# k's maximum over the partitions by TensorE transposes in the first three batches of an attention and feed-forward kernel

## The chip, the cores and the metric

The kernel runs on one core of a Trainium2 chip. The metric is device time in microseconds (us) of one execution. Engines carry the profile's names: PE is TensorE, DVE VectorE, ACT ScalarE, POOL GpSimd, SP SyncE (here the queue that issues every DMA). Each works through its own instructions in their order and waits on semaphores for the others.

## The reference

Linear attention, then a feed-forward block with softplus. q's softmax runs along each head's 64 columns, k's along the 576 rows of the sequence, and it is k's maximum over those rows that this case is about. The random inputs are scaled before use, q by 22.844, k, v and w_in by 8.

```python
batch, n_heads, seq, head_dim = (8, 8, 576, 64)
k_s = k - np.max(k, axis=2, keepdims=True)
k_s = np.exp(k_s)
k_s = k_s / (np.sum(k_s, axis=2, keepdims=True) + 1e-09)
kv = np.einsum('bhsd,bhse->bhde', k_s, v)
...
h = x @ w_in                     # x [4608, 512], w_in [512, 2048]
g = np.maximum(h, 0.0) + np.log1p(np.exp(-np.abs(h)))
return (g @ w_out).astype(np.float32)
```

## The kernel before

The 4608 tokens are cut into 12 tiles of 384, d_ff into 16 chunks of 128. One (tile, chunk) pair is a **slot**, and the 192 slots set the order of everything. In a slot TensorE makes `up` (x times a chunk of w_in, into PSUM tile `ph`), then `down` of two slots before (g times a chunk of w_out, into `po`), then what `later` has put aside: products of k and v and of x. ScalarE and VectorE make the softplus between (L405 to L411). Tile 0 takes the weights as float32; the other tiles take weights and x in two float32r parts (`hi` and `lo`), three products each.

The weights come as 32 loads of 512 KB of float64 bits and are made float32 on the chip, two chunks per slot of tile 0: GpSimd scales them (`scale_w`, L161), ScalarE takes the top bits (L166), VectorE the sign (L170) and the join (L177). From slot 6 on ScalarE (L190) and GpSimd (L191) also split two chunks per slot, into the place of chunks that tile 0 has used.

A `kv_unit` makes one head pair of one batch: `top` takes the maximum of k over the chunks (VectorE, tile `mx`) and then over the 128 partitions, the same result in every partition (GpSimd's `partition_all_reduce`, tile `mb`); `shift` subtracts it, on GpSimd for two head pairs of the first batch and for all units that tiles 1 and 2 plan, on VectorE else; `product` takes the exponential and multiplies by v and a column of ones; `scale` and `split` divide. x of a tile is `flip` (a 32x32 block transpose of q), `product` and `split`.

Before the first slot these steps stand in an order written out by hand (the string of names such as `u00` for step 0 of head pair 0, `q1`, `x00`, `w3`). In the slots a `Plan` places them: each step has a cost by engine, each unit a first slot (`KV_AT`) and a number of slots to wait after the step before, and the least room per slot that lets all fit is taken. Units of batch 1 are made in the slots of tile 0, two of batch 2 in tile 1. `kv_prefetch` loads the next head pair into one of two buffers once the products of an earlier one are done. All DMAs stand in SP's queue in program order; the load of tile 1's q (`q`) stands ahead of the weights from the fourth chunk on (`w3` and later), and waits until tile 0's q has been used.

Of the kernel before, what the change touches and what calls it, by code (L numbers as in the profile page):

```python
# [6 lines left out]

# [9 lines left out]
P = 128  # L17
B, H, S, D = 8, 8, 576, 64
DM, DF = 512, 2048
NT = B * S  # L20
HP = H // 2          # head pairs: one pair fills the 128 partitions
NJ = DF // P
NCH = S // P         # whole chunks of the sequence, plus one of half the rows
# [3 lines left out]
W_SCALE = 2.0**8     # what the weights on chip are scaled by  # L27
SPARE = 2            # see the weights

# Tiles of tokens of the feed-forward part, in blocks of 128. The first takes the weights as float32,  # L30
# while they are still being converted; the others take them, and all else, in two parts for float32r.
SUBS = [3] * 12
# From which slot (see slots()) the weights are split, and how many chunks of them in a slot.
SPLIT_FROM, SPLITS = 6, 2
# The slot from which the second tile's attention part is made.
ATT_FROM = 3
# When a tile comes to the products of k and v that it makes for the next, by their number.
KV_AT = {0: (), 1: (4,), 2: (2, 8), 3: (1, 5, 9), 4: (0, 2, 4, 6)}
# [10 lines left out]
def segments(t):  # L49
    """(batch, first column, last column) of the tokens of tile t."""  # L50
    out, a = [], START[t]
    while a < START[t + 1]:
        b = a // S
        e = min((b + 1) * S, START[t + 1])
        out.append((b, a - START[t], e - START[t]))
        a = e
    return out


def slots():  # L60
    """The order in which (tile, chunk of d_ff) go through the tensor engine."""
    return [(t, j) for t in range(NTILE) for j in range(NJ)]


class Plan:
    """Gives the steps of the work beside the feed-forward products their slots."""
# [6 lines left out]
    def place(self, unit, first, last, room):  # L73
        """Puts the steps of a unit, (slots to wait after the step before, cost by engine, function), where
        there is room for them, and returns their slots, or None."""
# [15 lines left out]
    def place_all(self, attempt):  # L91
        """attempt(plan, room) with the least room that does."""
# [11 lines left out]
def tile_attn_ffn(  # L104
    ctx: ExitStack,
    tc: tile.TileContext,
    q: bass.AP,       # [128, HP * NT]  tile after tile, in blocks of 32 x 32, see kernel()
    kv: bass.AP,      # [B, HP, 128, NCH, 2, 2 * D]  k and v of each head side by side
    kv_tail: bass.AP, # [B, HP, 64, 2, 2 * D]
    w_in: bass.AP,    # [NJ, 128, DM]  float64 as its 64 bits  # L110
    w_out: bass.AP,   # [NJ, 128, DM]  likewise
    out: bass.AP,     # [NT, DM]
# [20 lines left out]
    zero = const.tile([P, 1], F32, name="zero")  # L133
    ln1 = const.tile([P, 1], F32, name="ln1")

    # ---------------------------------------------------------------- weights
    # The weights of a chunk come as float64, and become float32 where they are. The first tile is made
    # from these. Then their two parts for float32r take the place of the chunk SPARE before.
# [12 lines left out]
    # A float64 has its sign, 11 bits of exponent and 20 of the fraction in the high word. Read as a  # L151
    # float32, scaled by 2^-111 and shifted left by 3, that word is the float32 of W_SCALE times the
    # value's magnitude without the fraction's last 3 bits, which are the top of the low word.
# [4 lines left out]
    def scale_w(i):  # L158
        """The high words, read as float32, by 2^-111."""
        _, high = words(i, F32)  # L160
        nc.gpsimd.tensor_scalar(out=high, in0=high, scalar1=2.0**-60, scalar2=2.0**-51, op0=ALU.mult, op1=ALU.mult)  # L161

    def top_w(i):
        """The low words' top 3 bits: the whole part of a 32nd of the top byte, to which the conversion rounds."""
        low, _ = words(i, U32)
        nc.scalar.activation(low, octets(i)[:, :, 3], AF.Copy, scale=1.0 / 32, bias=-15.5 / 32)  # L166

    def sign_w(i):
        """The sign, from the high words' top byte to that of the low words."""
# [4 lines left out]
    def join_w(i):  # L174
        """The float64 weights times W_SCALE, cut to float32, in the place of their low words."""
# [5 lines left out]
    def whole(i):  # L181
        """The weights of a chunk as float32, among the words that they came in."""
        return words(i, F32)[0]

    def split_w(i):
        """The two parts for float32r."""
# [7 lines left out]
    # ------------------------------------------------- k softmax and its product with v  # L194
    waiting = None  # where products that need not come at once are put
# [7 lines left out]
    KVW = 2 * D + 1  # a head's columns of k, its columns of v, a column of ones  # L203

    def kv_load(b, h, pool=kp, tag="kvt", shape=(P, NCH + 1, 2, KVW)):
# [3 lines left out]
        # Rows that the last chunk does not have: no maximum, weight 0.  # L209
# [9 lines left out]
    def kv_unit(b, h, ps, engine=nc.vector, after=None):  # L219
        """exp(k - max)' [v, 1] for one head pair, divided by its last column, as kv_hi and kv_lo."""  # L220
        t = loaded.pop((b, h))
        kt, vt = t[:, :, :, 0:D], t[:, :, :, D:KVW]
        ps = ps[:, 0:D + 1]
        state = {}

        def top():
            mx = sm.tile([P, 2, D], F32, name="mx")
            nc.vector.tensor_reduce(out=mx, in_=kt.rearrange("p c z d -> p z d c"), op=ALU.max, axis=AX.X)  # L228
            mb = sm.tile([P, 2, D], F32, name="mb")
# [5 lines left out]

        def shift():
            engine.tensor_tensor(
# [38 lines left out]
        return [top, shift, product, scale, split]  # L276

    def split_kv(h):
        """The two parts of a head pair's product in the first batch, which the first tile takes whole."""
# [3 lines left out]
    # ------------------------------------------------------------- q softmax, x  # L283
# [8 lines left out]
    def swapped(m):  # L292
        """The same columns of the other 32 partitions of the head."""
# [6 lines left out]
    def q_unit(t):  # L300
        """Softmax of q of tile t, two head pairs at a time."""
# [35 lines left out]
    def x_unit(t, h, ps, tiles=None):  # L337
        """x of a head pair, columns on the partitions and scaled by 1 / W_SCALE, in two parts but for tile 0."""
# [44 lines left out]
    # ------------------------------------------------------------ feed-forward  # L383
# [15 lines left out]
    def softplus(ph, t):  # L399
        """max(h, 0) + log1p(u), u = exp(-|h|); log1p(u) = ln(w) + (u - (w - 1)) with w = 1 + u."""  # L400
# [44 lines left out]
    def finish(t, m):  # L445
        """Writes out 128 tokens, after tile 0 by way of the places of the last weights that came."""
# [12 lines left out]
    # ---------------------------------------------------------------- schedule  # L459
# [12 lines left out]
    with tc.manual_schedule():  # L472
        # Before the first products much of what they need is free for their inputs to be made.
# [5 lines left out]
        for i in range(3):  # L479
            load_w(i)  # L480
        nc.vector.memset(zero, 0.0)
        # What the table gives for ln(1), so that log1p is exact where 1 + u rounds to 1.
# [6 lines left out]
        def place(h, at):  # L489
            """PSUM for a unit, in one of two banks."""  # L490
            return (more if h % 2 else att)[:, at:512]

        # Its parts step by step, in the order that lets every engine work: u for k and v, q, x and k
        # (split_kv) with their head pair and step, s and the like for the weights with their chunk.
# [16 lines left out]
        for name in (  # L511
# [152 lines left out]
```

## Time and profile before

| what | value |
|---|---|
| median of 3 runs | 1007.84 us (1007.72 to 1008.45) |
| profiled execution, its span | 1005.5 us |
| busy in the span | PE 90%, DVE 74%, ACT 61%, POOL 14% |
| first feed-forward product | 51.67 us |
| first product of tile 1 | 201.73 us |
| GpSimd's reductions | 32, from 7.28 us to 831.9 us |

The profile shows one execution. Its span runs from the first to the last recorded instruction; the time of a run lies a little above it. A bracket behind a row tells how long the engine had been idle and what ended that; "issue" means that the profile shows nothing it waited for. The page cuts the span into 40 slices of 25.1 us, the digit being the busy share in tenths: the first eight differ from all that follow.

```profile
PE   0297553889899999999999999999999999999998
DVE  7195566868678888788689788687888887676554
POOL 1322347434100000001000000001000000000000
PEclk9998875998999999999999999999999999999999
```

### The profile page before, as it was taken

Reading aid. Unit: us, or ns where it says so; the run is one execution under the profiler, and the core shown is the slowest. Engines: PE = TensorE matmul, PEld = TensorE weight load, DVE = VectorE, ACT = ScalarE, POOL = GpSimd, SP = SyncE. Lnnn points to the kernel's source line nnn. Section 1 sums busy time; section 2 is a strip of 40 time slices with the busy share of each in tenths; the row PEclk is TensorE's granted clock in tenths of the full one; section 3 lists DMA queues with packets and bytes.
Section 4 is the critical chain, followed back from the end, with each engine's and each line's share of the span. In section 5 each row is a group of like instructions: output and inputs, shape, how many; then the busy total and the mean of one; then the engine's idle time right before and its main releaser. Section 6 shows DMA issues by size and latency. Waiting matters only on the chain.

```text
span 1005.5 us, 13226 instructions
## 1 busy us (share of the span) xinstructions
PE 901.8 (90%) x4748; PEld 768.1 (76%) x4748; DVE 746.1 (74%) x1369; ACT 616.1 (61%) x1262; POOL 138.1 (14%) x205
## 2 busy tenths in 40 slices
PE   0297553889899999999999999999999999999998
PEld 0143222468798988989989888988988989999997
DVE  7195566868678888788689788687888887676554
ACT  2263334557566666676676676676667666666654
POOL 1322347434100000001000000001000000000000
PEclk9998875998999999999999999999999999999999
DMA  8273330100011101100110110110102001000000
GB/s 235 73 314 108 107 107 24 32 32 25 24 64 48 55 33 48 56 32 24 55 56 24 56 55 24 57 55 24 63 25 79 32 25 32 33 1 1 31 1 32
DMA packets 49473, 55.37 MB, mean 55 GB/s; under 512 B 2304, under 2 KB 39168, under 8 KB 49408
## 3 DMA queue, kind: packets, MB, share of 16 engines
q1 hardware_dynamic: 49408, 54.54, 16.6%
q8 instruction: 37, 0.61, 0.2%
q14 instruction: 28, 0.23, 0.1%
HBM read 45.09 MB, written 9.44 MB: 54 GB/s over the span
## 4 chain that ended last, share of the span: by engine, by line
PE 77%; issue 7%; DVE 6%; POOL 4%; DMA 3%; ACT 1%; SPq 0%; POOLq 0%; DVEq 0%
PE ph L394 12%; PE ph L396 12%; PE ph L395 12%; PE po L440 12%; PE po L441 12%; PE po L439 12%; DMA w<-in_w_in 3%; POOL w L191 2%; DVE w L177 1%; POOL w L161 1%; DVE w L170 1%; PE po L248 1%; PE po L435 1%; PE att L248 1%; DMA qt<-in_q 1%
## 5 line engine op out<-in xcount | busy, mean ns | idle before, releaser
L439 PE MATMUL po<-w,g_hi 128*128 128x512 f32 x528 | 206.5, 391 | 5.3 <-ACT g_hi L419 5.2
L394 PE MATMUL ph<-x_hi,w 128*128 128x384 f32 x616 | 210.4, 342 | 0.0
L441 PE MATMUL po<-w,g_lo 128*128 128x512 f32 x528 | 209.8, 397 | 0.0
L440 PE MATMUL po<-w,g_hi 128*128 128x512 f32 x528 | 209.3, 396 | 0.0
L396 PE MATMUL ph<-x_lo,w 128*128 128x384 f32 x616 | 208.0, 338 | 0.0
L395 PE MATMUL ph<-x_hi,w 128*128 128x384 f32 x616 | 207.2, 336 | 0.0
L409 DVE SCALAR_TENSOR_TENSOR w<-w,u 128x384 f32<-128x384 f32 x192 | 112.3, 585 | 126.7 <-ACT w L407 124.7
L419 ACT CAST g_hi<-l 128x384 fp32r<-128x384 f32 x176 | 90.5, 514 | 170.9 <-DVE l L411 170.6
L405 ACT ACTIVATE u<-ph 128x384 f32<-128x384 f32 x192 | 94.3, 491 | 60.7 <-PE ph L396 28.8
L410 DVE SCALAR_TENSOR_TENSOR u<-ph,w 128x384 f32<-128x384 f32 x192 | 107.1, 558 | 21.3 <-ACT q_hi L355 0.5
L394 PEld LDWEIGHTS ph<-x_hi,w 128*128 128x128 f32 x616 | 116.1, 188 | 5.7 <-issue 0.3
L395 PEld LDWEIGHTS ph<-x_hi,w 128*128 128x128 f32 x616 | 116.1, 189 | 4.4 <-issue 0.3
L439 PEld LDWEIGHTS po<-w,g_hi 128*128 128x128 f32 x528 | 99.7, 189 | 21.8 <-ACT g_hi L419 6.0
L441 PEld LDWEIGHTS po<-w,g_lo 128*128 128x128 f32 x528 | 99.4, 188 | 21.8 <-DVE g_lo L420 0.5
L396 PEld LDWEIGHTS ph<-x_lo,w 128*128 128x128 f32 x616 | 116.0, 188 | 0.0
L411 DVE SCALAR_TENSOR_TENSOR l<-l,ln,u 128x384 f32<-128x384 f32 x176 | 110.1, 625 | 6.3
L420 DVE TENSOR_TENSOR g_lo<-l,g_hi 128x384 fp32r<-128x384 f32 x176 | 97.6, 555 | 22.8 <-ACT g_hi L419 20.7
L440 PEld LDWEIGHTS po<-w,g_hi 128*128 128x128 f32 x528 | 99.6, 189 | 16.8
L406 ACT ACTIVATE u<-u 128x384 f32<-128x384 f32 x192 | 100.9, 526 | 6.1
L407 ACT ACTIVATE w<-u 128x384 f32<-128x384 f32 x192 | 100.8, 525 | 6.1
L230 POOL PARTITION_ALL_REDUCE mb<-mx x32 | 32.1, 1003 | 418.5 <-DVE mx L228 348.3
L408 ACT ACTIVATE l<-u 128x384 f32<-128x384 f32 x176 | 89.3, 508 | 0.0
(111 smaller groups left out, 1085.8 us busy)
## 6 DMA issues: line engine op xcount, KB each, us to landing
kvt<-in_kv SPq DMA_DIRECT2D x30, 512.0 KB, 4.3
qt<-in_q SPq DMA_DIRECT2D x12, 768.0 KB, 4.2
out<-w SPq DMA_DIRECT2D x33, 256.0 KB, 2.2
w<-in_w_in SPq DMA_DIRECT2D x16, 512.0 KB, 8.1
w<-in_w_out SPq DMA_DIRECT2D x16, 512.0 KB, 7.9
kvt<-in_kv_tail SPq DMA_DIRECT2D x30, 64.0 KB, 3.9
out<-x_lo SPq DMA_DIRECT2D x3, 256.0 KB, 3.2
x_hi<-in_kv SPq DMA_DIRECT2D x1, 512.0 KB, 8.5
```

The lines of the kernel that those rows point to most:

```text
L394: nc.tensor.matmul(ph, lhsT=w_hi, rhs=x_hi[:, h], start=h == 0, stop=False)
L395: nc.tensor.matmul(ph, lhsT=w_lo, rhs=x_hi[:, h], start=False, stop=False)
L396: nc.tensor.matmul(ph, lhsT=w_hi, rhs=x_lo[:, h], start=False, stop=h == HP - 1)
L406: nc.scalar.activation(u, u, AF.Exp, scale=-1.0)
L407: nc.scalar.activation(w, u, AF.Copy, bias=1.0)
L409: nc.vector.scalar_tensor_tensor(out=w, in0=w, scalar=1.0, in1=u, op0=ALU.subtract, op1=ALU.subtract)
L410: nc.vector.scalar_tensor_tensor(out=u, in0=ph, scalar=0.0, in1=w, op0=ALU.max, op1=ALU.subtract)
L411: nc.vector.scalar_tensor_tensor(out=l, in0=l, scalar=ln1, in1=u, op0=ALU.subtract, op1=ALU.add)
L420: nc.vector.tensor_tensor(out=g_lo, in0=l, in1=g_hi.bitcast(F32), op=ALU.subtract)
L439: nc.tensor.matmul(po, lhsT=g_hi[:, ms], rhs=w_hi, start=j == 0, stop=False)
L440: nc.tensor.matmul(po, lhsT=g_hi[:, ms], rhs=w_lo, start=False, stop=False)
L441: nc.tensor.matmul(po, lhsT=g_lo[:, ms], rhs=w_hi, start=False, stop=j == NJ - 1)
```

## The change

For batches 0 to 2 (`b <= ON_PE`) the maximum over the partitions is no longer taken on GpSimd. TensorE transposes `mx` into PSUM with an identity matrix, so that partitions become columns; VectorE takes the maximum of each row (`m1`, one column); TensorE transposes `m1`, read 128 times over, which puts all maxima into every partition. `shift` reads them from PSUM where VectorE does it; for GpSimd, ScalarE copies them into SBUF first. The middle piece is a new step, `across`, so the numbers of the later steps go up by one; for batches from 3 on it does nothing. The identity is made once on GpSimd. The order ahead of the first slot is written anew, and four units of a tile now begin at slots 0, 1, 4 and 5 instead of 0, 2, 4 and 6. Comments are also gone, which moves line numbers.

```diff
-KV_AT = {0: (), 1: (4,), 2: (2, 8), 3: (1, 5, 9), 4: (0, 2, 4, 6)}
+ON_PE = 2
+KV_AT = {0: (), 1: (4,), 2: (2, 8), 3: (1, 5, 9), 4: (0, 1, 4, 5)}
...
+    ident = const.tile([P, P], F32, name="ident")
...
-        ps = ps[:, 0:D + 1]
+        wide, ps = ps[:, 0:P], ps[:, 0:D + 1]
...
             nc.vector.tensor_reduce(out=mx, in_=kt.rearrange("p c z d -> p z d c"), op=ALU.max, axis=AX.X)
+            if b <= ON_PE:
+                later(lambda: nc.tensor.transpose(wide, mx.rearrange("p z d -> p (z d)"), ident))
+                return
             mb = sm.tile([P, 2, D], F32, name="mb")
             nc.gpsimd.partition_all_reduce(
...
+        def across():
+            if b > ON_PE:
+                return
+            m1 = sm.tile([P, 1], F32, name="m1")
+            nc.vector.tensor_reduce(out=m1, in_=wide, op=ALU.max, axis=AX.X)
+            later(lambda: nc.tensor.transpose(wide, m1.broadcast_to([P, P]), ident))
+
         def shift():
+            if b <= ON_PE:
+                mb = wide.rearrange("p (z d) -> p z d", z=2)
+                if engine is nc.gpsimd:
+                    mb = sm.tile([P, 2, D], F32, name="mb")
+                    nc.scalar.copy(mb.rearrange("p z d -> p (z d)"), wide)
+                state["mb"] = mb
...
-        return [top, shift, product, scale, split]
+        return [top, across, shift, product, scale, split]
...
+        make_identity(nc, ident)
...
-            "u00 u01 u10 q1 q0 u11 u12 q2 u20 q3 u21 q4 u30 u02 u13 q6 m2 q5 u03 t0 t2 q7 q9 u22 m1 u14 "
-            "q8 x00 x10 u31 x11 u32 u04 x30 x20 kv m0 s0 u33 x01 t1 s2 u23 u34 u24 x12 x31 kv s1 q w3 w4 "
-            "w5 w6 w7 j1 k0 k3 j0 j2 x02 m3 x32 x21 t3 t4 x22 k1 k2 m4"
+            "u00 u10 u01 u11 u20 u02 u21 u12 u30 u31 q0 q1 u22 u32 u03 u13 q2 m0 q3 m1 u04 u14 q4 u05 u15 "
+            "t0 q5 m2 t1 q6 u23 u33 q7 q9 q8 x00 u24 u34 x01 x10 x11 u25 u35 t2 x20 x30 kv s0 x21 x31 kv "
+            "j0 x02 x12 s1 q w3 w4 w5 w6 w7 j1 x22 x32 k0 k1 s2 m3 k2 k3 j2 t3 t4 m4"
...
                 costs = [
-                    (0, dict(dve=0.8, pool=1.3)), (1, dict(dve=0.75)), (1, dict(act=0.75)), (1, dict(dve=0.2)),
-                    (1, dict(dve=0.4, act=0.4)),
+                    (0, dict(dve=0.8, pool=1.3)), (1 if b <= ON_PE else 0, dict(dve=0.2 if b <= ON_PE else 0)),
+                    (1, dict(dve=0.75)), (1, dict(act=0.75)), (1, dict(dve=0.2)),
+                    (0 if b <= ON_PE else 1, dict(dve=0.4, act=0.4)),
                 ]
```

What the order of instructions becomes is shown at three places, before and then now. First GpSimd ahead of the first slot; `ISA mb<-mx` is the reduction, a bare `ISA` a change of configuration, `mb` and `mx` as above, `w_136` to `w_141` the first weights.

```order
L230 ISA
L230 ISA mb<-mx 128x128 x3
L237 ISA
L237 TENSOR_TENSOR x_hi<-x_hi,mb 128x10x64
L230 ISA
L230 ISA mb<-mx 128x128
L161 ISA
L161 TENSOR_SCALAR w_140<-w_140 128x512
L330 TENSOR_TENSOR qt<-qt,s 128x768
L161 TENSOR_SCALAR w_138<-w_138 128x512
L237 TENSOR_TENSOR x_lo<-x_lo,mb 128x10x64
```

```order
masks.py:197 MEMSET ident 128x128
masks.py:199 ISA
masks.py:199 AFFINE_SELECT ident<-ident 128x128
L258 TENSOR_TENSOR x_hi<-x_hi,mb 128x10x64
L258 TENSOR_TENSOR x_lo<-x_lo,mb 128x10x64
L165 TENSOR_SCALAR w_137<-w_137 128x512
L165 TENSOR_SCALAR w_139<-w_139 128x512
L165 TENSOR_SCALAR w_141<-w_141 128x512
L351 TENSOR_TENSOR qt<-qt,s 128x768
```

Four bare ISA rows have become one, ahead of the identity, and the subtractions, scalings and the multiply follow each other.

Second, VectorE at the same place (`m` and `m_171` are different tiles: the maxima of q, and the new column).

```order
L228 TENSOR_REDUCE mx<-kvt 128x128
L237 TENSOR_TENSOR kvt<-kvt,mb 128x10x64
L228 TENSOR_REDUCE mx<-kvt 128x128
L311 TENSOR_REDUCE m<-qt 128x24 x2
L237 TENSOR_TENSOR kvt<-kvt,mb 128x10x64
L297 COPY other<-m 32x48 x4
L314 TENSOR_TENSOR m<-m,other 128x48
L228 TENSOR_REDUCE mx<-x_hi 128x128
L317 TENSOR_TENSOR qt<-qt,m 128x768 x2
L228 TENSOR_REDUCE mx<-x_lo 128x128
```

```order
L232 TENSOR_REDUCE mx<-kvt 128x128 x2
L248 TENSOR_REDUCE m_171<-po_159 128x1
L248 TENSOR_REDUCE m_174<-po_160 128x1
L232 TENSOR_REDUCE mx<-x_hi 128x128
L258 TENSOR_TENSOR kvt<-kvt,po_159 128x10x64
L248 TENSOR_REDUCE m_181<-po_161 128x1
L258 TENSOR_TENSOR kvt<-kvt,po_160 128x10x64
L232 TENSOR_REDUCE mx<-x_lo 128x128
L248 TENSOR_REDUCE m_188<-po_162 128x1
L332 TENSOR_REDUCE m<-qt 128x24 x2
```

All four head pairs' maxima now stand ahead of the work on q.

Third, TensorE in tile 0, where batch 1 is made (`ph` is `up`, `po_415` and `po_432` and on `down`; `att` and `po_332` or `po_349` are the two banks of the units).

```order
L389 MATMUL ph<-x_hi,w_311 128x384 x4
L435 MATMUL po_415<-w_309,g_hi 128x512
L435 MATMUL po_416<-w_309,g_hi 128x512
L435 MATMUL po_417<-w_309,g_hi 128x512
L389 MATMUL ph<-x_hi,w_336 128x384 x4
L435 MATMUL po_415<-w_334,g_hi 128x512
L435 MATMUL po_416<-w_334,g_hi 128x512
L435 MATMUL po_417<-w_334,g_hi 128x512
L248 MATMUL att<-kvt 64x65 x10
```

```order
L234 MATMUL att<-ident,mx 128x128
L410 MATMUL ph<-x_hi,w_330 128x384 x4
L456 MATMUL po_432<-w_328,g_hi 128x512
L456 MATMUL po_433<-w_328,g_hi 128x512
L456 MATMUL po_434<-w_328,g_hi 128x512
L249 MATMUL att<-ident,m_483 128x128
L234 MATMUL po_349<-ident,mx 128x128
L410 MATMUL ph<-x_hi,w_353 128x384 x4
```

At the end of slots 3 to 5 TensorE's queue now has transposes, each behind a `mx` or `m1` of VectorE; the first head pair's products come at the end of slot 6, where they came at the end of slot 5.

More of the change, by code (lines that the diff above doesn't have):

```diff
@@ L6 @@
 from concourse._compat import with_exitstack
+from concourse.masks import make_identity
 F32 = mybir.dt.float32
```

## The prediction

> **What bounds the kernel now.** I read the profiled execution by stages first: up to the first feed-forward product, tile 0, and the rest.
>
> ```profile
> core 0: us, PE busy (x) PEld busy (x) DVE busy (x) ACT busy (x) POOL busy (x), PEclk, DMA share, GB/s
> 201.70:1005.50 803.80, 791.83 (x4346) 708.91 (x4344) 613.38 (x1159) 533.70 (x1100) 56.59 (x104) 0.99 0.12 38
> 51.60:201.70 150.10, 99.07 (x315) 52.44 (x316) 108.51 (x158) 70.14 (x139) 67.16 (x68) 0.82 0.32 112
> 0.00:51.60 51.60, 10.90 (x88) 6.75 (x88) 24.21 (x54) 12.22 (x25) 14.31 (x34) 1.00 0.54 161
> ```
>
> From 201.70 us on TensorE is busy for 791.83 of 803.80 us: that is the bound, and little can be won there. Tile 0 is another matter: in 150.10 us no engine is full (VectorE 108.51, TensorE 99.07 at a granted clock of 0.82), and before it the busiest, VectorE, works less than half the time. Next, who waits for whom between 75 and 250 us, and the events recorded at the reduction's line:
>
> ```profile
> DVE w L170 <- POOL w L161: 31.8, 8, 11.5
> POOL w L161 <- issue: 27.3, 4, 6.9
> ACT w L190 <- POOL w L191: 45.7, 8, 16.8
> L230 POOL PARTITION_ALL_REDUCE mb<-mx x32: 703/934/2274, 7.3 to 831.9; - x32
> L230 POOLq MODIFY_POOL_CONFIG  x18: 2/11/19, 3.0 to 263.5; - x18
> ```
>
> VectorE's conversion of the weights waits 31.8 us for GpSimd, and GpSimd 27.3 us for "issue", for nothing that the profile names. The reduction itself takes 0.7 to 2.3 us; beside it stand configuration events, the last pair at 263.5. The chain of waits gives the price of such a switch, and GpSimd's timeline more of them:
>
> ```profile
> 27.68 5.51 issue
> 33.19 0.72 POOL mb L230
> ...
> 33.97 6.80 issue
> 40.77 0.63 POOL w L161
> ```
>
> ```profile
> 7.28 0.70 POOL L230 PARTITION_ALL_REDUCE mb<-mx  x1 [4.26 <-DVE mx L228]
> 119.77 0.72 POOL L230 PARTITION_ALL_REDUCE mb<-mx  x1 [10.12 <-issue]
> 127.35 1.89 POOL L161 TENSOR_SCALAR w<-w 128x512 f32<-128x512 f32 x2 [6.85 <-issue]
> 329.82 0.94 POOL L230 PARTITION_ALL_REDUCE mb<-mx  x1 [7.14 <-DVE mx L228]
> ```
>
> Into the reduction a switch costs from under 4.3 us (the first, hidden behind mx) to 10.1, out of it 6.8. GpSimd's ordinary work, the scaling of the weights (L161) above all, is queued behind; VectorE's sign and join wait for that, and TensorE for these.
>
> **The change part by part.** The three batches have 12 head pairs. Their twelve reductions go, and with them every switch up to 264 us but one, ahead of the identity's AFFINE_SELECT. A second stands ahead of batch 3's reductions, where GpSimd has no other arithmetic left; it is hidden, as the row at 329.82 is, behind the wait for VectorE's mx.
>
> Added: 24 transposes, 12 VectorE maxima over 128 columns (m1), 8 ScalarE copies of 128 columns, the identity. Rows for their prices and for work that moves (timeline; groups of the first 60 us; the rows of tile mb; the page):
>
> ```profile
> 81.83 0.97 PE L248 MATMUL att<-kvt 128*64 128x65 f32 x20 [1.88 <-ACT kvt L243]
> L258 DVE TENSOR_SCALAR r<-po 128x1 f32<-128x1 f32 x4 | 0.7, 164 | 0.0
> L410 DVE SCALAR_TENSOR_TENSOR u<-ph,w 128x384 f32<-128x384 f32 x1 | 0.6, 557 | 0.1
> L170 DVE TENSOR_SCALAR w<-w 128x512 uint8<-128x512 uint8 x6 | 4.5, 784 | 2.5 <-POOL w L161 2.5
> L177 DVE SCALAR_TENSOR_TENSOR w<-w 128x512 uint32<-128x512 uint32 x5 | 4.7, 980 | 0.0
> L237 DVE TENSOR_TENSOR kvt<-kvt,mb x24: 817/820/827, 8.0 to 834.6; 128x640 f32<-128x640 f32 x24
> L405 ACT ACTIVATE u<-ph 128x384 f32<-128x384 f32 x192 | 94.3, 491 | 60.7 <-PE ph L396 28.8
> 58.56 2.86 PE L389 MATMUL ph<-x_hi,w 128*128 128x384 f32 x8 [1.48 <-DVE u L410]
> ```
>
> A transpose of 128 columns lies between one 65-column pass (0.97/20 = 0.05 us) and two 384-column passes (2 x 2.86/8 = 0.72). I take 0.3, a little over two passes in proportion to width, so 7.2 us for the 24. m1 lies between 0.16 (one column) and 0.56 (384 columns out of PSUM); a third of the way is 0.29, twelve of them 3.5 us. A copy takes less than the 0.49 of 384 columns; ScalarE, 70.14 us busy of 150.10 in tile 0, hides it.
>
> By the Trainium skill (TensorE: Matmul & The Clock Gate, Part 4: PE-mode transpose) a 128x128 bf16 transpose takes 390 ns alone and about 275 ns inside a kernel; 24 at 390 ns would be 9.4 us. No run here shows one yet.
>
> *The start.* VectorE now makes both mx of the first two head pairs, their two m1, then mx of x_hi. That one waits for its load, so the identity matters only where it comes later than the load.
>
> ```profile
> 4.53 0.56 SPq L213 DMA_DIRECT2D x_hi<-in_kv  x1
> x_hi<-in_kv SPq DMA_DIRECT2D x1, 512.0 KB, 8.5
> 10.72 1.81 DVE L311 TENSOR_REDUCE m<-qt 128x24 f32<-128x768 f32 x2 [0.57 <-DMA qt<-in_q]
> 23.91 0.54 DVE L347 STREAM_TRANSPOSE u<-qt 128x384 f32<-128x384 f32 x1
> 42.99 0.58 DVE L347 STREAM_TRANSPOSE g_lo<-qt 128x384 f32<-128x384 f32 x1 [18.54 <-POOL qt L330]
> 44.47 5.29 DMA w<-in_w_in
> 51.26 0.83 POOL L161 TENSOR_SCALAR w<-w 128x512 f32<-128x512 f32 x1 [0.63 <-DMA w<-in_w_out]
> 51.67 5.41 PE L389 MATMUL ph<-x_hi,w 128*128 128x384 f32 x16
> ```
>
> x_hi lands at 4.53 + 8.5 = 13.0, and its tail is issued right behind: 13.4. The identity: memsets to 3.0, where the first configuration event stands, a switch of 6.8, a select that I put at L161's 0.63: 10.4. So it costs 0. With a switch of 10.1 it is ready at 13.7, and transposes and two m1 end near 15, a loss of 2; a quick switch gains nothing, for the load is later. From 10.72 to 24.45 VectorE was packed, 13.7 us. The same work runs after 13.4, with one shift (0.8), two m1 (0.6), two more r with their reciprocals (0.6) and some 0.5 of waiting for transposes: to 29.6. The two flips that had waited 18.54 us for GpSimd's multiply follow at once (2 x 0.54), since no switch is ahead of it: 30.8. The last x product (two passes at the 0.76 of the row at 201.73 below) and its copy (0.5) put the first feed-forward product at 33, not 51.67.
>
> What is late next is the weights' DMA. On SP the load of q waits for those flips, and all weights from the fourth chunk stand behind it. It goes at 30.9, the first weight 0.4 later, landing after 5.29 us at 36.6; the next is 1.4 behind (GpSimd takes it up at 51.26, and the first was there at 49.76). Scaling 0.83, a sign 0.78, two joins 1.96 and two operations of slot 0's softplus, 1.1, put slot 2 at 42.7 against 58.56. With the slots from there to 74.51 at their old pace, **15.9 us** are kept.
>
> *Tile 0, slots 5 to 15*, 127.2 us in all:
>
> ```profile
> 74.51 2.74 PE L389 MATMUL ph<-x_hi,w 128*128 128x384 f32 x8
> 169.88 5.05 PE L389 MATMUL ph<-x_hi,w 128*128 128x384 f32 x8
> 201.73 0.76 PE L394 MATMUL ph<-x_hi,spare 128*128 128x384 f32 x1
> 74.50:201.70 127.20, 77.73 (x258) 41.17 (x257) 86.54 (x126) 55.12 (x108) 60.51 (x60) 0.79 0.23 75
> ```
>
> Without VectorE's 31.8 us of waiting, and with four m1 (1.2), 96.6 remain: the upper value. The four slots from 169.88 hold no reduction and take 31.85, 8.0 each; eleven are 88, the lower value, just over VectorE's own 86.54 + 1.2. I take 92: **35.2 us** less. Each transpose stands at the end of a slot in TensorE's queue and waits for mx or m1, with the next slot's product behind it. VectorE makes these first in its slot, and TensorE's 77.73/11 = 7.1 us per slot leave 1.3 of the 8.4 for it; without that cover each transpose could cost up to the 1.3 of a mx. The third and fourth head's loads now come one slot before their mx: a slot of 8 covers them, and a late one would show as VectorE waiting for DMA.
>
> *After tile 0* two stalls go:
>
> ```profile
> 227.63 0.79 PE L439 MATMUL po<-w,g_hi 128*128 128x512 f32 x1 [5.24 <-ACT g_hi L419]
> 261.85 0.80 PE L248 MATMUL po<-kvt 128*64 128x65 f32 x20 [3.17 <-ACT kvt L243]
> 222.30:232.80 10.50, 5.26 (x30) 3.74 (x29) 4.17 (x6) 6.87 (x13) 8.41 (x7) 0.67 0.00 0
> ```
>
> That is 5.24 + 3.17, and about 2 for the clock of 0.67 behind the first; batch 2's eight transposes lie on the bound and take 2.4 back. **8.0 us** net.
>
> Sum: 15.9 + 35.2 + 8.0 = 59.1; 1005.5 - 59.1 = 946.4 of span. The median of 1007.84 is 2.3 more than the span: 948.7.
>
> **The rivals.** *Tile 0 stays slow.* ScalarE's copies wait 45.7 us for GpSimd's splits, which wait for these copies in turn, and VectorE's 31.8 us were partly cover for that. If half of them comes back (16 us) and the start loses 4, it is 969. For it: the slots from 169.88 take 8.0 without any reduction. Against: the longest of those waits, 16.8, has the switch at 119.77 to 127.35 in it.
>
> *More is won.* From 58.56 to 74.51 three slots took 5.3 each. Were the others near 6, eleven would be 66, 26 less than I take: 923. Against it stand VectorE's 86.54 us; for it, that sum holds operations stretched beside GpSimd's bursts after a switch.
>
> *Slower.* TensorE and VectorE run in step: a transpose that waits for VectorE holds the next product back, and softplus with it. Tile 0 has eight such places; at 59.1/8 = 7.4 us each, a whole slot of VectorE, the gain is gone, and at 10 it is 1007.8 + 8 x 2.6 = 1029. Against it: the 7.1 of 8.4 above, and two banks that take turns.
>
> *The switches were hidden.* With its code in place the reduction has a median of 0.93; two transposes and m1 are 0.9 and two hand-overs more. If the "issue" time had cost nothing, the change wins nothing and pays up to its 7.2 us of transposes: 1008 to 1015. The rows at 33.97 and 127.35, on the way to the weights that VectorE waits for, speak against it. The Trainium skill (GPSIMD Engine Reference, 4.1 Engine selection) names GPSIMD for a reduction along the partitions; by that rule the work moves the wrong way, and the gap of 6.85 us after a 0.72 us reduction is what its table leaves out.
>
> **How the numbers follow.** The forecast, 948.7, has 64%; its own range is 936 to 963, from 88 to 96.6 for tile 0, the start 3 us either way and the rest 4. Tile 0 stays slow 19%, more is won 11%, slower 4%, hidden 2%. The range 928 to 973 takes in the slow case around 969 and the nearer part of the better one. A measurement of this kernel tells about 0.2% from no change. Faster 0.95, same 0.01, slower 0.04.
>
> **What would show it.** No "issue" gap near 6.8 us on GpSimd before 250 us but the identity's; the first feed-forward product near 33, slot 2 near 43, tile 1 near 151; signs that no longer wait for GpSimd's scaling. I am wrong if mx of x_hi starts after 16 us, if TensorE waits over 20 us in tile 0 for mx or m1, or if the slots from the fifth on average under 7 or over 9 us.

## The result, and the profile after

The change takes 962.01 us (median of 4 runs, 959.32 to 962.28) against 1007.88 us (1007.72 to 1008.45): a ratio of 0.9543, 95% interval 0.9527 to 0.9559. The forecast was 948.7, so the direction and the range held, and the gain was 13 us smaller than forecast. The profiled execution has a span of 960.2 us.

The page of the kernel after, again in 40 slices, now of 24.0 us:

```profile
PE   2597778989999999999999999999999999999998
DVE  5799999886887897886896896886896896776554
POOL 2334746510000000010000000000000000000000
PEclk9998899999999999999999999999999999999999
```

VectorE's row has become full where TensorE's was thin: slices 3 to 7 now read 9 for VectorE, and slices 5 to 7, which read 5, 5 and 3 for TensorE, read 7, 7 and 8. The stages (from, to, length, then busy time of each engine, the granted clock and the DMA share), cut at the first feed-forward product, at slot 2, at slot 5 and at tile 1's first product:

```profile
core 0: us, PE busy (x) PEld busy (x) DVE busy (x) ACT busy (x) POOL busy (x), PEclk, DMA share, GB/s
38.90:49.20 10.30, 5.33 (x17) 2.95 (x15) 6.22 (x13) 6.73 (x15) 4.87 (x6) 0.99 1.01 403
49.20:68.36 19.16, 18.31 (x46) 9.06 (x46) 18.66 (x27) 11.00 (x23) 4.92 (x6) 0.92 0.78 311
68.36:164.40 96.04, 76.20 (x265) 40.15 (x264) 89.25 (x127) 53.41 (x109) 55.26 (x53) 0.89 0.28 88
164.40:960.20 795.80, 789.60 (x4354) 706.03 (x4352) 618.65 (x1163) 534.72 (x1103) 51.02 (x100) 1.00 0.12 38
```

Slots 5 to 15 took 127.2 us and take 96.04; VectorE is busy for 89.25 of them. GpSimd's waits between 68.4 and 164.4 us hold no "issue" any more, and VectorE no longer waits for its scalings. Against the forecast's stages:

| stage | before | forecast | after | after less forecast |
|---|---|---|---|---|
| up to the first product | 51.67 | 33 | 38.90 | +5.9 |
| from there to slot 2 | 6.9 | 9.7 | 10.30 | +0.6 |
| slots 2 to 4 | 15.95 | 15.9 | 19.16 | +3.2 |
| slots 5 to 15 | 127.2 | 92 | 96.04 | +4.0 |
| after tile 0 | 803.8 | 795.8 | 795.80 | 0.0 |
| median less span | 2.3 | 2.3 | 1.8 | -0.5 |

But for rounding the last column adds up to the 13.3 us between 948.7 and 962.0. Nearly ten of them are lost before slot 5. The three places that the forecast named for the profile were missed with it: the first product came at 38.90 and not near 33, slot 2 at 49.20 and not near 43, tile 1 at 164.40 and not near 151.

### The profile page after: what moved, and what is told of

The parts are those of the page before. It is cut to its first block, busy times and chain, and to the rows that moved or that the text cites. A ratio compares the mean times of both kernels' runs of the same rounds, so it can differ in the third digit from the quotient of the medians.

```text
span 960.2 us, 13251 instructions
## 1 busy us (share of the span) xinstructions
PE 902.8 (94%) x4772; PEld 766.9 (80%) x4772; DVE 757.7 (79%) x1381; ACT 617.7 (64%) x1270; POOL 126.6 (13%) x195
## 4 chain that ended last, share of the span: by engine, by line
PE 80%; DVE 12%; DMA 2%; ACT 2%; issue 1%; POOL 1%; SPq 0%; DVEq 0%; ACTq 0%
PE ph L415 13%; PE po L461 12%; PE po L462 12%; PE ph L417 12%; PE ph L416 12%; PE po L460 12%; DMA w<-in_w_out 2%; DVE w L181 2%; DVE w L174 2%; DVE w L430 1%; DVE mx L232 1%; DVE u L431 1%; PE po L269 1%; PE att L269 1%; DVE other L318 1%
## 5 line engine op out<-in xcount | busy, mean ns | idle before, releaser
L237 POOL PARTITION_ALL_REDUCE mb<-mx x20 | 19.9, 993 | 308.7 <-DVE mx L232 302.0
```

## The experiments

The theory to test: the gain is that of GpSimd's switches into and out of the reduction; what the start lost against the forecast is the identity's switch and the order of ScalarE's work; tile 0 is now VectorE's. The rivals: the rewritten order makes the gain; transposes that wait for VectorE set tile 0's pace; the switches were hidden. The times below are medians, each with its ratio to runs of the kernel before on the same chip and the 95% interval. Those runs had medians from 1006.42 to 1007.88 us, so a difference of one or two microseconds between two of the times says little. The last three columns are of one profiled execution each.

| kernel | time | ratio to before | first product | tile 0 from there | after tile 0 |
|---|---|---|---|---|---|
| before | 1007.88 | 1 | 51.67 | 150.1 | 803.8 |
| the change | 962.01 | 0.9543 (0.9527 to 0.9559) | 38.90 | 125.5 | 795.8 |
| before, reductions made copies | 946.27 | 0.9394 (0.9352 to 0.9436) | 33.1 | 117.6 | 794.3 |
| new order alone | 992.02 | 0.9848 (0.9798 to 0.9898) | 36.9 | 150.0 | 802.2 |
| batch 0 on TensorE | 992.18 | 0.9850 (0.9799 to 0.9900) | 37.4 | 148.9 | 805.1 |
| batches 0 and 1 | 967.97 | 0.9609 (0.9535 to 0.9684) | 36.2 | 125.7 | 801.8 |
| batches 1 and 2 | 962.61 | 0.9557 (0.9535 to 0.9579) | 37.39 | 127.8 | 796.0 |
| old order, batches 0 to 2 | 957.67 | 0.9511 (0.9487 to 0.9535) | 38.59 | 123.1 | 795.8 |

### The kernel before without a switch

```diff
-            nc.gpsimd.partition_all_reduce(
-                mb.rearrange("p z d -> p (z d)"), mx.rearrange("p z d -> p (z d)"), channels=P,
-                reduce_op=bass_isa.ReduceOp.max,
-            )
+            nc.gpsimd.tensor_copy(mb.rearrange("p z d -> p (z d)"), mx.rearrange("p z d -> p (z d)"))
```

> The kernel before, in its old order, with each reduction over the partitions replaced by a GpSimd copy of the same 128 columns (the maximum over the partitions is left out, so each partition subtracts its own). No transposes, no new order. If the switches of GpSimd's configuration carried the cost: span 950 to 970, no 'issue' gap near 6.8 us, first feed-forward product near 33 us. If the new order or the new place of the work carried the gain: above 990.

Measured 946.27, a little below the range expected. GpSimd still runs one instruction per head pair, 0.58 us each, where the reduction took 0.7 to 2.3, and 61 us are gone, far more than those instructions differ by. So this is, but for that difference, the price of all the switches in the kernel before, and it is more than the change wins: with nothing added to other engines, tile 0 takes 117.6 us, and 125.5 with the transposes.

### The new order alone, and TensorE batch by batch

```diff
-ON_PE = 2
+ON_PE = -1
-        make_identity(nc, ident)
```

> The changed kernel with all reductions on GpSimd again, in the new order ahead of the first slot and with the new KV_AT, without the identity. If the switches carry the cost: 1000 to 1025, close to the kernel before or worse, since the new order still puts GpSimd's arithmetic between reductions. If the order carried the gain: 960 to 980.

Measured 992.02, between the two: with every reduction still on GpSimd, the rewritten order alone wins about 15 us (10 to 20 by its interval), and its first product comes earlier than that of the whole change. GpSimd's timeline of this kernel says why:

```profile
7.10 0.70 POOL L237 PARTITION_ALL_REDUCE mb<-mx  x1 [4.10 <-DVE mx L232]
...
17.01 0.70 POOL L237 PARTITION_ALL_REDUCE mb<-mx  x1 [0.82 <-DVE mx L232]
25.60 1.44 POOL L258 TENSOR_TENSOR x_hi<-x_hi,mb 128x640 f32<-128x640 f32 x1 [7.89 <-DVE s L342]
...
127.80 0.72 POOL L237 PARTITION_ALL_REDUCE mb<-mx  x1 [5.92 <-issue]
136.87 1.88 POOL L165 TENSOR_SCALAR w<-w 128x512 f32<-128x512 f32 x2 [8.35 <-issue]
```

Batch 0's four reductions stand in one group, from 7.10 to 17.71, with one switch behind them, where the old order had three: out, in again for the fourth, and out. In tile 0 the switches are all still there, of 5.92 and 8.35 us in the last rows, and tile 0 takes 150 us as before.

```diff
-ON_PE = 2
+ON_PE = 0
```

> The changed kernel with only batch 0 on TensorE (ON_PE = 0): batches 1 and 2 reduce on GpSimd. By the switches: what the start is worth alone, some 12 us off the kernel before, 990 to 1000; tile 0 has four reductions again with gaps of 6 to 10 us on both sides. If the gain of tile 0 came from elsewhere: under 980.

Measured 992.18. The number was met, but it is also that of no batch on TensorE (992.02): taking batch 0's reductions off GpSimd, once they stand together, wins nothing that these runs show.

```diff
-ON_PE = 2
+ON_PE = 1
```

> The changed kernel with batches 0 and 1 on TensorE (ON_PE = 1); batch 2 reduces on GpSimd. By the prediction's last term batch 2 is worth 8.0 us: 970. If batch 2's transposes on the bound cost as much as its two stalls: 962.

Measured 967.97 (its two runs, 965.34 and 970.6, lie far apart). Batch 1 alone makes a step of 24 us between the medians, nearly all of it in tile 0 (148.9 to 125.7 in the profiled executions); batch 2 then takes 801.8 to 795.8 after tile 0, 6.0 us, where 8.0 were forecast. Slots 5 to 15 took 127.2 us before, 122.0 with the new order alone, 121.1 with batch 0 on TensorE and 95.5 with batch 1. So of the 35.2 us forecast there the switches of batch 1 bring 25.6, and some 5 more came with the new order.

Putting batch 0 back on GpSimd and leaving batches 1 and 2 on TensorE is the same question from the other side:

```diff
-ON_PE = 2
+ON_PE = (1, 2)
...
-        make_identity(nc, ident)
+        todo["id"] = lambda: make_identity(nc, ident)
...
-            "u00 u10 u01 u11 u20 u02 u21 u12 u30 u31 q0 q1 u22 u32 u03 u13 q2 m0 q3 m1 u04 u14 q4 u05 u15 "
+            "u00 u10 u01 u11 u20 u02 u21 u12 u30 id u31 q0 q1 u22 u32 u03 u13 q2 m0 q3 m1 u04 u14 q4 u05 u15 "
```

> Only batches 1 and 2 go over TensorE. Batch 0's four reductions are GpSimd's again, one behind the other, and the identity is made right after the fourth. If the start lost its time to the switch ahead of the identity (10.4 us, with three engines waiting for it), that switch now stands where the one back from the reductions stands anyway: first product at 36.9, as in the kernel that has only the new order, and 959 to 960. If batch 0 gains by TensorE what I forecast (no switch between it and the weights' scaling), it is 3 to 7 us slower than 962.

Measured 962.61, the change's own time within its spread: neither the gain of 2 us nor the loss of 3 to 7 that I had forecast for batch 0. The first product, 37.39, lies within the 36.1 to 38.9 that the kernels with the same written order, the identity ahead and single transposes show.

### The old order with TensorE

```diff
-KV_AT = {0: (), 1: (4,), 2: (2, 8), 3: (1, 5, 9), 4: (0, 1, 4, 5)}
+KV_AT = {0: (), 1: (4,), 2: (2, 8), 3: (1, 5, 9), 4: (0, 2, 4, 6)}
...
-            "u00 u10 u01 u11 u20 u02 u21 u12 u30 u31 q0 q1 u22 u32 u03 u13 q2 m0 q3 m1 u04 u14 q4 u05 u15 "
...
+            "u00 u01 u02 u10 q1 q0 u11 u12 u13 q2 u20 q3 u21 u22 q4 u30 u03 u14 q6 m2 q5 u04 t0 t2 q7 q9 u23 "
...
```

> The three batches on TensorE, but with the order and the first slots of the units of the kernel before (each new step stands just ahead of its shift). Tile 0 and the rest have no switch in either. If the switches were what made the start slow, and the new order and TensorE are two ways to lose them, the first product comes near 33.1 (old order without switches) plus up to 8 that VectorE now waits for the identity, 34 to 41, and the time is 958 to 966. If the written order itself made the start quick, it stays near 51.67: about 975.

Measured 957.67, with the first product at 38.59. So the old order was not slow in itself: the new order and TensorE are two ways to lose the same switches at the start, and their gains do not add. The old order with TensorE enters slot 5 at 63.89, the change at 68.36, and takes 97.76 us for slots 5 to 15 against 96.04. It is if anything faster than the change; the intervals, 0.9487 to 0.9535 and 0.9527 to 0.9559, still overlap a little.

### One more pair of switches

```diff
+                if n == 9:
+                    more_mx = sm.tile([P, 16], F32, name="more_mx")
+                    more_mb = sm.tile([P, 16], F32, name="more_mb")
+                    nc.vector.memset(more_mx, 0.0)
+                    nc.gpsimd.partition_all_reduce(more_mb, more_mx, channels=P, reduce_op=bass_isa.ReduceOp.max)
```

> One reduction on GpSimd of 16 columns, whose result nobody reads, is added in slot 9 of tile 0, and with it one switch into the reduction and one out of it. If the switches are the price (the four reductions of batch 1 cost 24 us of tile 0 between the kernels with one and with two batches on TensorE), it costs about 6 us, 4 to 10: 966 to 972, with a gap of 5 to 10 us ahead of it and 6.8 behind. If only the reduction's own 0.7 us and the wait for its result cost (which nobody reads here): 962 to 963.

GpSimd's timeline of this kernel:

```profile
101.82 2.90 POOL L195 TENSOR_TENSOR w<-w,w 128x512 fp32r<-128x512 f32 x2 [3.99 <-ACT w L194]
110.96 0.95 POOL L636 PARTITION_ALL_REDUCE more_mb<-more_mx  x1 [6.24 <-DVE w L174]
119.04 1.44 POOL L258 TENSOR_TENSOR kvt<-kvt,mb 128x640 f32<-128x640 f32 x1 [7.13 <-issue]
```

Both gaps are there, 6.24 and 7.13 us, for a reduction that nobody reads. The first is not all switch: GpSimd stood still from 104.72 on, and VectorE set the reduction's operand only at 108.18, so 3.5 us of it would have been waited in any case. The second ends at "issue" and is clean. Measured 964.78 (ratio 0.9591, 0.9569 to 0.9613), 2.8 us over the change, 4.8 by the ratios; in the profiled execution slots 5 to 15 take 100.4 instead of 96.0, 4.4 more. The sign is the theory's and the size the low end of the range expected or below it: 13.4 us in which GpSimd stands cost 3 to 5. The four pairs of batch 1 cost 24, 6 each. That GpSimd, busy for 55 of those 96 us, works off a single gap and not four would explain the difference; no run tests it.

### The price of a transpose

```diff
-                later(lambda: nc.tensor.transpose(wide, mx.rearrange("p z d -> p (z d)"), ident))
+                later(lambda: [nc.tensor.transpose(wide, mx.rearrange("p z d -> p (z d)"), ident) for _ in range(3)])
-            later(lambda: nc.tensor.transpose(wide, m1.broadcast_to([P, P]), ident))
+            later(lambda: [nc.tensor.transpose(wide, m1.broadcast_to([P, P]), ident) for _ in range(3)])
```

> Each of the 24 transposes is done three times, one after the other; the result is the same. If a transpose costs its TensorE time only where TensorE is the bound, batch 2's 16 extra ones at the 0.27 us of their shortest row cost 4.3 us, and those of batches 0 and 1 hide in TensorE's idle time: 966. If TensorE and VectorE go in step in tile 0 (the rival called slower), all 48 extra ones count at the median of 0.45 us: 962 + 21.6 = 983. If none counts: 962.

Measured 965.35 (0.9584, 0.9556 to 0.9613), near the 966 of the theory and far from the 983 of a TensorE and VectorE in step. That the number fits 966 is luck: after tile 0 the 16 more take 797.1 - 795.8 = 1.3 us, not 4.3, and the rest comes where the theory had nothing, 1.2 us ahead of the first product (40.09) and 1.5 in slots 5 to 15. The 1.3 us stand out: the change and the four other kernels that do the same work after tile 0 (the added reduction, the exponentials ahead, batch 0 on GpSimd, the old order) take 795.7 to 796.1 there.

```diff
-ON_PE = 2
+ON_PE = 7
```

> All eight batches go over TensorE: 40 more transposes, 20 more m1, and no reduction on GpSimd at all. If a transpose costs its 0.27 us on the bound after tile 0: 962 + 10.8 = 973. By the price that tripling them showed there (16 more in 1.3 us more, 0.08 each): 965. If the switches after 264 us had been hidden for nothing, it cannot be under 961.

Measured 965.04 (0.9588, 0.9568 to 0.9607), the 965 of the price just found. The stage after tile 0:

```profile
162.53:962.80 800.27, 793.84 (x4394) 708.09 (x4392) 619.52 (x1183) 534.50 (x1104) 31.24 (x80) 1.00 0.12 38
```

40 more transposes and 20 more m1 take 4.5 us more than the change's 795.80, 0.11 for each transpose if m1 costs nothing. They win nothing there, which fits reductions that from batch 3 on were hidden behind VectorE's mx. This kernel has no reduction at all, and shows one thing more. GpSimd's timelines, of this kernel, of the change and of the one with batches 1 and 2:

```profile
3.21 0.29 POOL masks.py:199 TENSOR_SCALAR_AFFINE_SELECT ident<-ident 128x128 f32<-128x128 f32 x1
```

```profile
13.61 0.28 POOL masks.py:199 TENSOR_SCALAR_AFFINE_SELECT ident<-ident 128x128 f32<-128x128 f32 x1 [10.47 <-DMA x_hi<-in_kv_tail]
```

```profile
18.35 0.29 POOL masks.py:199 TENSOR_SCALAR_AFFINE_SELECT ident<-ident 128x128 f32<-128x128 f32 x1
```

Without a reduction in the program the select comes at once; with one it waits 10.47 us for a switch (the DMA that the bracket names is not the cause: the same gap, 10.50 us in the kernel with tripled transposes, ends at "issue"); right behind reductions it waits for nothing. And yet the kernel with the select at 3.21 has its first product at 36.17, those with it at 11.3 to 11.8 at 36.1 to 37.4, and the change, at 13.61, at 38.90: an identity that is there before the load of x_hi (13.4) costs nothing.

### The start and ScalarE's order

```diff
-            "u00 u10 u01 u11 u20 u02 u21 u12 u30 u31 q0 q1 u22 u32 u03 u13 q2 m0 q3 m1 u04 u14 q4 u05 u15 "
-            "t0 q5 m2 t1 q6 u23 u33 q7 q9 q8 x00 u24 u34 x01 x10 x11 u25 u35 t2 x20 x30 kv s0 x21 x31 kv "
+            "u00 u10 u01 u11 u20 u02 u21 u12 u30 u31 q0 q1 u22 u32 u03 u13 q2 m0 q3 m1 u04 u14 q4 q5 q6 m2 "
+            "u05 u15 u23 u33 t0 t1 q7 q9 q8 x00 u24 u34 x01 x10 x11 u25 u35 t2 x20 x30 kv s0 x21 x31 kv "
```

> In the order ahead of the first slot q's exponentials, sums and the two steps around them stand ahead of the copies and byte conversions that stood before them on ScalarE; nothing else moves. If that queue on ScalarE made 2 us of the late start (VectorE's sum over q waited 1.71 us for the exponential), the first feed-forward product comes at 36 to 37 and not 38.90 and the time is 959 to 960. If the late start is the identity's and the transfers' alone: 962.

Measured 959.22 (0.9525, 0.9500 to 0.9550), in the range expected, though the interval overlaps that of the change. The first product comes at 33.19, earlier than expected; the identity's select, at 11.71, was 1.9 us earlier too. The trace is clearer than the time. ScalarE and VectorE of the change, then VectorE of the kernel that has this edit and the next one:

```profile
25.58 1.29 ACT L289 ACTIVATE spare<-po,r 64x64 f32<-64x64 f32 x4 [3.62 <-DVE r L279]
26.89 0.65 ACT L170 ACTIVATE w<-w 128x512 uint32<-128x512 uint8 x1
27.45 0.82 ACT L341 ACTIVATE qt<-qt 128x768 f32<-128x768 f32 x1
```

```profile
28.31 0.95 DVE L342 TENSOR_REDUCE s<-qt 128x24 f32<-128x768 f32 x1 [1.71 <-ACT qt L341]
...
35.02 0.54 DVE L368 STREAM_TRANSPOSE g_lo<-qt 128x384 f32<-128x384 f32 x1
```

```profile
24.08 1.95 DVE L342 TENSOR_REDUCE s<-qt 128x24 f32<-128x768 f32 x2
...
30.81 0.54 DVE L368 STREAM_TRANSPOSE g_lo<-qt 128x384 f32<-128x384 f32 x1
```

In the change q's exponential stands behind four copies (1.29), which themselves waited 3.62 us for VectorE, and a byte conversion (0.65). With it ahead VectorE's sums follow without a wait, the last flip begins at 30.81 (the forecast had the flips end at 30.8), and the first product at 33.19 and 32.82 (forecast 33). From the identity's select to the first product it is 25.3 us in the change, 21.5 and 21.2 with the exponentials ahead. By slot 5 the lead of 5.7 us has shrunk to 3.8 (64.59 against 68.36), for the weights are late next: TensorE waits 6.77 us ahead of slot 2 where it waited 4.98 in the change.

### Splitting the weights later

```diff
-SPLIT_FROM, SPLITS = 6, 2
+SPLIT_FROM, SPLITS = 12, 2
```

> The weights are split from slot 12 of tile 0 on and not from slot 6. If tile 0 is bound by VectorE and VectorE's operations are stretched beside GpSimd's splits (L181 1.73 us each against 0.98), slots 6 to 11 lose about 1 us each: 954 to 957, as long as tile 1 finds its weights in time. If the waits of TensorE for mx and m1 set tile 0's pace, nothing changes: 962. If the splits come too late for tile 1 (24 chunks are then split beside it), it waits for them: above 966.

Measured 955.72 (0.9494, 0.9461 to 0.9527). Its slots 5 to 15 and the stage after tile 0, then VectorE's groups in slots 5 to 15, of this kernel and of the change (count, busy us, mean ns):

```profile
66.18:151.83 85.65, 70.06 (x264) 36.89 (x264) 79.02 (x126) 46.39 (x96) 36.92 (x41) 0.96 0.30 99
151.83:952.30 800.47, 790.77 (x4354) 705.66 (x4352) 625.29 (x1163) 541.40 (x1116) 72.02 (x112) 1.00 0.12 38
```

```profile
L181 DVE SCALAR_TENSOR_TENSOR w<-w 128x512 uint32<-128x512 uint32 x21 | 18.1, 900 | 0.0
L174 DVE TENSOR_SCALAR w<-w 128x512 uint8<-128x512 uint8 x21 | 16.5, 883 | 0.0
```

```profile
L181 DVE SCALAR_TENSOR_TENSOR w<-w 128x512 uint32<-128x512 uint32 x21 | 23.5, 1157 | 0.0
L174 DVE TENSOR_SCALAR w<-w 128x512 uint8<-128x512 uint8 x21 | 19.0, 1005 | 0.0
```

Slots 5 to 15 take 85.65 instead of 96.04, 10.4 us less, and VectorE's busy time falls by as much, 89.25 to 79.02, though it does the same 126 or so instructions: the same 21 joins take 900 ns each instead of 1157. The edit moves ScalarE's half of the split (L194) as well as GpSimd's (L195), but the rows of the change tell them apart:

```profile
73.05 1.30 DVE L181 SCALAR_TENSOR_TENSOR w<-w 128x512 uint32<-128x512 uint32 x2
```

```profile
94.49 3.50 POOL L195 TENSOR_TENSOR w<-w,w 128x512 fp32r<-128x512 f32 x2 [5.13 <-ACT w L194]
95.08 3.46 DVE L181 SCALAR_TENSOR_TENSOR w<-w 128x512 uint32<-128x512 uint32 x2
```

Two joins with GpSimd idle take 1.30 us, two that begin beside GpSimd's splits 3.46. Of the 21 joins in slots 5 to 15, seven run beside no GpSimd instruction and take 668 to 733 ns, three of these with ScalarE at work (695 to 733); eight begin beside a GpSimd operation with two inputs, six times a split and twice a shift, and take 1747 to 1922. So in slots 5 to 15 VectorE is the busiest engine, and GpSimd's work at its side slows it. The splits are then made in tile 1, at 4.7 us (800.47 against 795.80).

Both edits together, the later split and the exponentials ahead (the two diffs above in one kernel):

> Both edits together: q's exponentials ahead on ScalarE, and the weights split from slot 12 on. If they act at different places (the start, and slots 6 to 11 of tile 0), their gains add: the later split alone measured 955.72, the other order alone 959.22 against 962.01, so about 953, with slot 5 near 64.6 and tile 0's slots 5 to 15 near 86 us. If both only uncover the same limit, the arrival of the weights: 956.

Measured 952.77, ratio 0.9468 (0.9447 to 0.9488): the gains add, slot 5 starts at 64.10 and slots 5 to 15 take 85.6. This version beats both kernels.

## Why the prediction was right, and where it was not

**The bound and the direction: right.** Tile 0 was held up by GpSimd's switches: batch 1 alone is worth 24 us, copies in place of all reductions 61. *The switches were hidden* has fallen. The Trainium skill (GPSIMD Engine Reference, 2.1 Instruction dispatch) tells of some 6 us at the first call to freshly loaded code, with no visible instruction; the gaps that end at "issue", 5.92 us ahead of a reduction and 7.13 behind the one that nobody reads, are near it, and show that it is paid in both directions and each time anew. The Trainium skill's choice of GpSimd for a reduction along the partitions (the same page, 4.1 Engine selection) holds here only where the switch is hidden: from batch 3 on, where TensorE was 3 us slower, 965.04 against 962.01.

**The start, 15.9 us: the step that failed.** Measured 74.51 - 68.36 = 6.2. Three things were off in its working.

- *"The same work runs after 13.4 ... to 29.6."* It counted VectorE's work alone. ScalarE's exponentials stood behind copies and a conversion: 3.8 to 4.1 us from the select on, by the kernels with the exponentials ahead, which come to the forecast's 33. Another 2 us came from the identity: the forecast put its switch at 6.8 and named 10.1 with a loss of 2 as the other case; it was 8.2 to 10.5 from kernel to kernel, and this one drew 10.5.
- *"With the slots from there to 74.51 at their old pace"*: 19.16 us and not 15.95. Half of the 3.2 us is slot 2. TensorE begins it after a wait of 4.98 us (1.48 before), and its first eight products, at a granted clock of 0.62, take 4.28 us instead of 2.69 at 1.00; the new order alone shows the same, 4.33 at 0.61 after a wait of 4.79. The other half is slots 3 and 4. There TensorE, busy throughout before, has three transposes more and stands for 0.85 us, and VectorE is busy for 11.82 of 12.18. VectorE has a second mx and a second maximum of q there, but so has the new order alone, which keeps the old 10.56; what it has not is m1 and the transposes, behind which the next product waits. So this is the rival *Slower* in small, and neither it nor the clock was in the sum of the start.
- The order had no place in the sum. Two things, each alone, take all or most of the start's switches away: the new order with its reductions on GpSimd enters slot 5 at 64.92, TensorE with the old order at 63.89. The change has both and enters it at 68.36 (74.51 before). I credited TensorE alone with the start and had made no rival of the order.

Slot 2, then slots 3 and 4, of the kernel before, of the new order alone and of the change (for the first and the last also slot 2's first eight products), with the columns of the stages above:

```profile
58.56:61.25 2.69, 2.69 (x8) 1.68 (x9) 2.69 (x4) 1.51 (x4) 1.65 (x2) 1.00 1.03 410
58.56:63.95 5.39, 5.39 (x14) 2.81 (x15) 5.25 (x8) 3.10 (x6) 1.65 (x2) 1.00 1.03 410
63.95:74.51 10.56, 10.56 (x29) 5.39 (x28) 10.20 (x17) 6.18 (x12) 0.73 (x1) 1.00 0.55 218
```

```profile
47.27:54.36 7.09, 7.09 (x15) 3.54 (x15) 6.95 (x11) 4.39 (x10) 2.00 (x3) 0.76 1.03 407
54.36:64.92 10.56, 10.56 (x30) 5.39 (x28) 10.20 (x17) 6.25 (x13) 1.62 (x1) 1.00 0.51 203
```

```profile
49.20:53.48 4.28, 4.28 (x9) 2.44 (x10) 4.28 (x5) 3.30 (x7) 2.68 (x4) 0.62 1.03 410
49.20:56.18 6.98, 6.98 (x15) 3.57 (x16) 6.84 (x9) 3.56 (x8) 4.11 (x6) 0.77 1.03 410
56.18:68.36 12.18, 11.33 (x33) 5.49 (x31) 11.82 (x19) 7.43 (x16) 0.81 (x1) 1.00 0.64 254
```

**Tile 0, slots 5 to 15, 92 us: mis-sized, inside its bounds.** 96.04, at the upper value of 96.6, which was what stayed when VectorE's 31.8 us of waiting were taken out. The lower value took the last four slots, at 8.0, for all eleven. They take 7.7 now, but slots 6 to 11 take 9.5: VectorE is busy for 8.9 us of each against 7.0 in the last four, and 85.65 for all eleven is what is left when the splits are moved out of them. The Trainium skill (SBUF — State Buffer, SBUF: two separate sides) tells of a pair of ports that GpSimd and a VectorE instruction with two SBUF inputs, or in a two-port mode, take in turns, each for a whole instruction. The joins, which have two inputs, agree, with 668 to 733 ns alone and 1747 to 1922 beside a GpSimd operation that has two; the signs, with one, stretch as well, 883 to 1005, and no run shows in which mode they go.

**After tile 0, 8.0 us: right in the sum, not in its terms.** 795.80 as forecast. A transpose on the bound costs about 0.1 us of time and not 0.3, so batch 2's eight take 0.9 and not 2.4; taking its switches away won 6 net against the kernel with batches 0 and 1. The other 2 us were there before batch 2 moved, and the kernels that leave batch 2 on GpSimd lie 3 us apart in that stage (801.8 to 805.1), so they are not explained, and that the sum came out to the tenth is luck.

**The prices.** m1 was put at 0.29, and is. The transposes ran as follows (shortest, median, longest in ns), between the bounds of 0.05 and 0.72, and the first group's median half as long again as the 0.3 taken; the Trainium skill's 275 ns for bf16 inside a kernel (TensorE: Matmul & The Clock Gate, Part 4: PE-mode transpose) is about that of the shortest rows here, in float32:

```profile
L234 PE MATMUL po<-ident,mx x8: 275/448/477, 13.9 to 267.3; 128*128 128x128 f32 x8
L234 PE MATMUL att<-ident,mx x4: 271/302/389, 61.7 to 249.4; 128*128 128x128 f32 x4
L248 DVE TENSOR_REDUCE m<-po x8: 279/287/292, 14.5 to 269.0; 128x1 f32<-128x128 f32 x8
```

**The rivals.** *Slower* needed 7.4 us for each of eight waits; in tile 0 TensorE's products waited 9.0 us in all for mx and m1, its weight loads 13.8 (waits of the products from 68.4 to 164.4 us: total, times, longest), and tripling the transposes changed little:

```profile
PE po L249 <- DVE m L248: 4.7, 2, 2.6
PE att L249 <- DVE m L248: 2.1, 1, 2.1
PE po L234 <- DVE mx L232: 1.8, 2, 1.0
PE att L234 <- DVE mx L232: 0.4, 1, 0.4
```

*Tile 0 stays slow* gave 969, nearer to 962 than the forecast itself, but its mechanism did not occur: VectorE waits for GpSimd's scalings no more, and ScalarE's copies' wait for the splits did not hand its cover back as a wait; what kept tile 0 above the forecast was VectorE's own work, longer beside GpSimd's. *More is won* would have needed 66 us in slots 5 to 15; even without the splits in slots 6 to 11 it is 85.65. Of what I had named as proof against me, nothing occurred: mx of x_hi started at 14.88, TensorE waited 9.0 to 13.8 us and not 20, and the slots from the fifth took 96.04/11 = 8.7.

**The range.** The terms given for 936 to 963 (88 to 96.6 for tile 0, 3 us for the start, 4 for the rest) add up to 938 to 960 around 948.7. By its own terms the forecast's case thus ended just below 962, and it was the start, off by 9.7 us where 3 were allowed, that went beyond them. The measured time lies one microsecond inside the stated upper end.

## What to carry to other kernels

Where an engine stands idle at "issue" around one kind of instruction, count the changes to and from that kind, not the instructions: grouping four reductions won as much at the start as taking them off the engine. When a stall goes, price the stretch behind it anew before keeping "the old pace": what the change puts there on each engine, which product then waits behind it, and the clock that is granted after a wait. And follow the operands through every engine's queue, not only that of the busiest. Where a change comes with a rewritten order, cost the order alone as a rival.

## What the runs showed that was not expected

- The identity's select waited 8.2 to 10.5 us in the kernels that have a reduction anywhere, and did not wait in the one that has none and in the one where a reduction stands right ahead.
- A transpose that takes 0.27 to 0.48 us by its own row costs about 0.1 us of time on a stretch where TensorE is busy for 99% of it (16 more in 1.3 us, 40 more in 4.5). Where the rest of a row goes was not tried.
- The granted clock rose with TensorE's busy share of slots 5 to 15: 0.79 at 61% before, 0.89 at 79% in the change, 0.96 at 82% with the splits moved away.
